# Value products of an attention kernel moved to 64x64 and 32-row tiles of the TensorE array, with smaller weight casts in the ramp

## The chip, the cores and the metric

The kernel runs on one core of a Trainium2 chip. The metric is device time in microseconds (us) of one execution, as median of several; the profile of one of them gives the span, which is about 1.7 us shorter.

## The reference

Eight batches, eight heads, 576 queries, head dimension 64. K and V are averaged over eight neighbours, which leaves 72 keys per head; the attention's output goes through a two-layer MLP of width 2048.

```python
k_p = k.reshape(B, H, Sp, 8, D).mean(axis=3)          # Sp = 72
v_p = v.reshape(B, H, Sp, 8, D).mean(axis=3)
attn = softmax(q @ k_p^T / sqrt(D))
x = (attn @ v_p), heads side by side                  # 4608 x 512
out = gelu_tanh(x @ w_in) @ w_out                     # w_in 512 x 2048, w_out 2048 x 512
```

## The kernel before

Tokens come in nine groups of 512: groups 0 to 7 hold 512 queries of one batch each, and a remainder group R holds the last 64 of every batch; it runs before group 7. TensorE works through group g's MLP while the attention of the next group is slipped in between, at numbered slots ("hooks"). The eight heads' 72 weights each lie side by side in 576 rows, cut into five chunks of 128, the first of which is half empty, so a head's rows straddle two chunks. The pooled V (`vbd`) is stored once for every pair of heads and chunk, with a mask that zeroes the rows of other heads. One pair's value product is then two full-array matmuls, most of whose rows are zeros or other heads' blocks:

```python
PARTS = {0: [(0, 0), (1, 1)], 1: [(1, 2), (2, 3)], 2: [(2, 4), (3, 5)], 3: [(3, 6), (4, 7)]}  # (chunk, vbd slot)

def values(g, half, eng):                     # called twice per group: half 0, then half 1
    xo = psum.tile([128, 2, MAIN], F32, name="xo", tag="sc", bufs=2)
    for i in range(2):
        pr = 2 * half + i
        for x, (c, n) in enumerate(PARTS[pr]):            # groups 1 to 7
            nc.tensor.matmul(out=xo[:, i, :], lhsT=vbd[:, g, n, :], rhs=eT[:, :, c, :],
                             start=(x == 0), stop=(x == 1))
        # ... (remainder group: 64 columns at a time)
    copy(eng, st[g]["xT"][:, 2 * half:2 * half + 2, :], xo)      # eng is ScalarE

def hidden(g, fo, hook, s):                   # 16 per group
    for ko in range(KO):                                  # KO = 4 slices of xT
        hook(s + ko)
        nc.tensor.matmul(out=hp, lhsT=w_in_b[:, ko, ...], rhs=st[g]["xT"][:, ko, :], ...)
    nc.scalar.activation(out=gT[:, fo, :], in_=hp, func=ACT.Gelu_apprx_tanh)
```

Here `eT` holds a group's transposed softmax weights, `xo` its value products and `xT` their copy that the MLP reads; `kbd`, met later, is its pooled K as the score matmuls read it. After a group's value products come the last output matmuls of the group before (four for group 1, seven for the others), and then `hidden` reads `xT`. The ramp (group 0 and the first weights) is a chain of its own: warm-up matmuls, pooling of K by TensorE (`vp`), scores, softmax on VectorE, value products in halves, and GpSimd casting w_in as it lands. In the ramp, the slots are

```python
warm_up(34, "mm")
# ...
at(hooks, 80, cast_q, 1, 0, 2, nc.gpsimd)     # group 1's q, the half that is transposed first
at(hooks, 80, cast_q, 1, 2, 4, nc.vector)
# ...
at(hooks, [114, 118, 122, 125][j], q_transpose_pe, 1, j, nc.vector, "sc")
```

The softmax here doesn't subtract the row's maximum and nothing guards it: scores larger than these inputs give would overflow.

## Time and profile before

| | before |
|---|---|
| median of the first 3 runs | 298.57 us |
| span of the profiled run | 296.90 us |
| TensorE busy | 288.5 us, 97% |
| value products, groups 1 to 7 | 56 matmuls, 1.73 us of path per group |
| stretch from one group's value products to the next | 29.72 (group 1), 30.35 (groups 2, 3, 5), 30.48 (group 4) |
| TensorE's longest waits in the ramp, once its warm-up has begun at 1.43 us | 0.81 us for the K transfer, 0.79 and 0.69 for VectorE's softmax, 0.48 and 0.23 for w_in casts |

"Stretch" is the measure to follow: from the first value matmul of a group to that of the next. The lines themselves stand in the prediction. In them PE is TensorE and PEld its weight loads, DVE is VectorE, ACT ScalarE, POOL GpSimd, and SPq the queue of SyncE, which issues transfers.

### The profile page before, as it was taken

Reading aid. Unit: us, or ns where it says so; the run is one execution under the profiler, and the core shown is the slowest. Engines: PE = TensorE matmul, PEld = TensorE weight load, DVE = VectorE, ACT = ScalarE, POOL = GpSimd, SP = SyncE. Lnnn points to the kernel's source line nnn. Section 1 sums busy time; section 2 is a strip of 40 time slices with the busy share of each in tenths; the row PEclk is TensorE's granted clock in tenths of the full one; section 3 lists DMA queues with packets and bytes.
Section 4 is the critical chain, followed back from the end, with each engine's and each line's share of the span. In section 5 each row is a group of like instructions: output and inputs, shape, how many; then the busy total and the mean of one; then the engine's idle time right before and its main releaser. Section 6 shows DMA issues by size and latency. Waiting matters only on the chain.

```text
span 296.9 us, 4533 instructions
## 1 busy us (share of the span) xinstructions
PE 288.5 (97%) x1716; PEld 149.3 (50%) x1716; DVE 140.3 (47%) x234; ACT 155.9 (52%) x229; POOL 63.3 (21%) x82
## 2 busy tenths in 40 slices
PE   6889999999999999999999999999999999999996
PEld 6668854445444544454445444544444544444445
DVE  5873768165527561747065807481729100920012
ACT  1475584777066706671567256724773367427500
POOL 3564433231303040304002400240024000100000
PEclk9999999999999999999999999999999999999999
DMA  7999997995699269936994599059944600451012
GB/s 235 356 386 342 382 365 204 345 253 156 139 307 299 58 137 290 264 112 135 276 257 148 125 265 288 1 116 249 278 143 102 167 36 2 83 111 35 2 71 71
DMA packets 73301, 56.32 MB, mean 190 GB/s; under 512 B 45888, under 2 KB 55488, under 8 KB 73280
## 3 DMA queue, kind: packets, MB, share of 16 engines
q1 hardware_dynamic: 73136, 55.98, 67.9%
q8 instruction: 13, 0.21, 0.3%
q10 hardware_dynamic: 144, 0.07, 0.1%
q14 instruction: 8, 0.07, 0.1%
HBM read 36.70 MB, written 9.44 MB: 155 GB/s over the span
## 4 chain that ended last, share of the span: by engine, by line
PE 91%; DMA 4%; SPq 3%; POOL 1%; issue 0%; DVE 0%
PE mm L326 41%; PE mm L310 37%; PE xo L280 4%; PE mm L321 4%; DMA w_in_s<-in_moe_w_in_dram 4%; PE sc L213 2%; SPq L403 2%; PE mm L354 1%; POOL w_in_b L80 1%; SPq L98 1%; PE xo L286 1%; SPq L110 0%; PE sc L220 0%; PE tp L198 0%; PE xo L269 0%
## 5 line engine op out<-in xcount | busy, mean ns | idle before, releaser
L326 PE MATMUL mm<-w_out_b,gT 128*128 128x512 bf16 x560 | 128.7, 379 | 0.0
L310 PE MATMUL mm<-xT,w_in_b 128*128 128x512 bf16 x512 | 111.8, 379 | 0.0
L312 ACT ACTIVATE gT<-mm 128x512 bf16<-128x512 f32 x128 | 76.5, 597 | 41.8 <-PE mm L310 41.8
L326 PEld LDWEIGHTS <-gT 128*128 128x128 bf16 x560 | 53.4, 98 | 58.5
L310 PEld LDWEIGHTS <-w_in_b 128*128 128x128 bf16 x512 | 50.1, 98 | 60.5
L80 DVE COPY osb<-mm 128x512 f32<-128x512 f32 (+2 forms) x37 | 24.2, 658 | 60.9 <-PE mm L326 58.7
L78 ACT CAST xT<-xo 128x1024 bf16<-128x1024 f32 (+1 forms) x18 | 16.6, 967 | 57.5 <-PE xo L280 47.8
L235 DVE TENSOR_REDUCE den<-e 128x8 f32<-128x576 f32 x36 | 26.5, 736 | 41.6 <-ACT e L228 41.6
L153 POOL TENSOR_TENSOR vbd<-kvb,vmask 128x256 bf16<-128x256 bf16 (+2 forms) x40 | 21.2, 553 | 104.9 <-DVE kvb L133 104.7
L131 DVE TENSOR_TENSOR kv<-kv 128x1024 f32<-128x1024 f32 (+3 forms) x19 | 21.8, 1147 | 33.8 <-DMA kv<-in_v_dram 30.0
L228 ACT ACTIVATE e<-sc 128x576 f32<-128x576 f32 x36 | 22.4, 650 | 9.7 <-ACT e L228 5.8
L240 DVE TENSOR_TENSOR eb<-e,r 128x576 bf16<-128x576 f32 x26 | 24.4, 940 | 0.9
L80 POOL CAST q_b<-q_sb 128x2048 bf16<-128x2048 f32 (+2 forms) x9 | 17.1, 1897 | 14.6 <-DMA q_sb<-in_q_dram 8.5
L240 POOL TENSOR_TENSOR eb<-e,r 128x576 bf16<-128x576 f32 x6 | 6.9, 1149 | 61.3 <-ACT e L228 34.1
L321 PE MATMUL mm<-xT,w_in_b 128*128 128x256 bf16 x128 | 15.9, 273 | 0.7 <-POOL w_in_b L80 0.7
L213 PEld LDWEIGHTS <-qT 128*128 128x128 bf16 x128 | 10.0, 98 | 7.2 <-issue 0.4
L213 PE MATMUL sc<-kbd,qT 128*128 128x144 bf16 x128 | 13.1, 226 | 0.3 <-ACT qT L78 0.2
L321 PEld LDWEIGHTS <-w_in_b 128*128 128x128 bf16 x128 | 12.0, 98 | 2.6 <-POOL w_in_b L80 1.3
L280 PE MATMUL xo<-eT,vbd 128*128 128x512 bf16 x56 | 13.2, 379 | 0.0
L132 DVE TENSOR_TENSOR kv<-kv 128x512 f32<-128x512 f32 (+3 forms) x19 | 12.4, 651 | 0.7
L323 ACT ACTIVATE gT<-mm 128x512 bf16<-128x512 f32 x16 | 9.4, 597 | 5.2 <-PE mm L321 5.2
L520 ACT ACT_TABLE_LOAD x8 | 10.3, 1283 | 0.1
(59 smaller groups left out, 124.7 us busy)
## 6 DMA issues: line engine op xcount, KB each, us to landing
out_dram<-osb SPq DMA_DIRECT2D x31, 256.0 KB, 6.7
kv<-in_k_dram SPq DMA_DIRECT2D x7, 1024.0 KB, 7.4
q_sb<-in_q_dram SPq DMA_DIRECT2D x7, 1024.0 KB, 6.3
kv<-in_v_dram SPq DMA_DIRECT2D x6, 1024.0 KB, 8.9
w_in_s<-in_moe_w_in_dram SPq DMA_DIRECT2D x8, 512.0 KB, 10.4
w_out_s<-in_moe_w_out_dram SPq DMA_DIRECT2D x4, 1024.0 KB, 13.7
kv<-in_v_dram SPq DMA_DIRECT2D x4, 512.0 KB, 10.2
out_dram<-osb SPq DMA_DIRECT2D x9, 128.0 KB, 2.3
```

The costliest lines, as they stand in the source:

```text
L80: eng.tensor_copy(out=out, in_=in_)
L131: add(out=t[:, :, 0:4, :], in0=t[:, :, 0:4, :], in1=t[:, :, 4:8, :], op=ALU.add)
L153: eng.tensor_tensor(out=vbd[p0:128, b, n0:n1, :].rearrange("p (c r) (hh d) -> p c (r hh) d", c=max(m, 1), d=D), in0=kvb[p0:128, 4 + c0:4 + ...
L213: nc.tensor.matmul(out=o, lhsT=qT[:, j, pr, :], rhs=kbd[:, g, pr].rearrange("d hh s -> d (hh s)"), start=True, stop=True)
L228: nc.scalar.activation(out=e.rearrange("p (x h) s -> p x (h s)", x=2), in_=sc[:, :, 0:4 * Sp], func=ACT.Exp, scale=1.0 / 64.0)
L235: nc.vector.reduce_sum(out=den, in_=e, axis=AX.X)
L240: eng.tensor_tensor(out=o.rearrange("p (h s) -> p h s", s=Sp), in0=e, in1=r.unsqueeze(2).to_broadcast([128, H, Sp]), op=ALU.mult)
L280: nc.tensor.matmul(out=xo[:, i, :], lhsT=vbd[:, g, n, :], rhs=eT[:, :, c, :], start=(x == 0), stop=(x == 1))
L310: nc.tensor.matmul(out=hp, lhsT=w_in_b[:, ko, fo * 128:(fo + 1) * 128], rhs=st[g]["xT"][:, ko, :], start=(ko == 0), stop=(ko == KO - 1))
L312: nc.scalar.activation(out=gT[:, fo, :], in_=hp, func=ACT.Gelu_apprx_tanh)
L321: nc.tensor.matmul(out=hp[:, f, :], lhsT=w_in_b[:, ko, (fo + f) * 128:(fo + f + 1) * 128], rhs=st[g]["xT"][:, ko, c0:c0 + 256], start=(ko ...
L326: nc.tensor.matmul(out=o, lhsT=gT[:, fo, r * 128:(r + 1) * 128], rhs=w_out_b[:, fo, :], start=(fo == 0), stop=(fo == FO - 1))
```

## The change

The intent is to use the array's empty part. A head's 72 rows are split in a block of at most 64 rows and a rest of at most 32, at row offsets that the array can take as a tile; sixteen small matmuls then replace eight large ones, and four on different tiles can run side by side. Smaller w_in casts and earlier slots for group 0's second value products are meant to shorten TensorE's waits in the ramp.

```diff
+    BIG = [(64, 0), (0, 1), (64, 1), (0, 2), (0, 3), (64, 3), (0, 4), (64, 4)]        # per head: first row, chunk
+    SMALL = [(0, 1), (64, 1), (0, 2), (64, 2), (96, 2), (32, 3), (96, 3), (32, 4)]
-    def values(g, half, eng):
+    def values(g, eng):
+        xo = [psum.tile([128, 2, MAIN], F32, name="xo", tag="sc", bufs=2) for _ in range(2)]
+            for part, rows_ in ((SMALL, 32), (BIG, 64)):
+                for i in range(2):
+                    for pr in (i, i + 2):
+                        for hh in range(2):
+                            r0, c = part[2 * pr + hh]
+                            n = dict(PARTS[pr])[c]
+                            nc.tensor.matmul(out=xo[i][64 * hh:64 * hh + 64, pr // 2, :],
+                                             lhsT=vbd[r0:r0 + rows_, g, n, 64 * hh:64 * hh + 64],
+                                             rhs=eT[r0:r0 + rows_, :, c, :], start=(part is SMALL), stop=(part is BIG))
 ... (remainder group: as before, pairs in the order 0, 2, 1, 3)
+            copy(eng, st[g]["xT"].rearrange("p (y i) t -> p i y t", i=2)[:, i], xo[i])
 ...
-        for ko in range(KO):
+        for i, ko in enumerate([0, 2, 1, 3]):
 ...
-        cast_w_in(c, 2, nc.gpsimd)
+        cast_w_in(c, 2, nc.gpsimd, 0, 256)
+        cast_w_in(c, 2, nc.gpsimd, 256, 512)
 ...
-    at(hooks, 32, first_t, 3)
-    at(hooks, 38, first_v)
+    at(hooks, 26, first_t, 3)
+    at(hooks, 32, first_v)
```

More of the change, by code (lines that the diff above doesn't have):

```diff
@@ L271, in values_half @@
         copy(eng, st[g]["xT"][:, 2 * x:2 * x + 2, 256 * half:256 * half + 256], xo)
-    def values(g, half, eng):
-        xo = psum.tile([128, 2, MAIN], F32, name="xo", tag="sc", bufs=2)
+    BIG = [(64, 0), (0, 1), (64, 1), (0, 2), (0, 3), (64, 3), (0, 4), (64, 4)]
+    SMALL = [(0, 1), (64, 1), (0, 2), (64, 2), (96, 2), (32, 3), (96, 3), (32, 4)]
+    def values(g, eng):
+        xo = [psum.tile([128, 2, MAIN], F32, name="xo", tag="sc", bufs=2) for _ in range(2)]
         eT = st[g]["eT"]
-        for i in range(2):
-            pr = 2 * half + i
-            if g < B:
-                for x, (c, n) in enumerate(PARTS[pr]):
-                    nc.tensor.matmul(out=xo[:, i, :], lhsT=vbd[:, g, n, :], rhs=eT[:, :, c, :],
-                                     start=(x == 0), stop=(x == 1))
-            else:
-                for b in range(B):
-                    p0 = 64 * (b % 2)
-                    for x, (c, n) in enumerate(PARTS[pr]):
-                        nc.tensor.matmul(out=xo[:, i, 64 * b:64 * b + 64], lhsT=vbd[:, b, n, :],
-                                         rhs=eT[:, b // 2, c, p0:p0 + 64], start=(x == 0), stop=(x == 1))
-        copy(eng, st[g]["xT"][:, 2 * half:2 * half + 2, :], xo)
@@ new lines, in values @@
+        if g < B:
+            for part, rows_ in ((SMALL, 32), (BIG, 64)):
[7 more added lines that the diff above has]
+                                             rhs=eT[r0:r0 + rows_, :, c, :], start=(part is SMALL), stop=(part is BIG))
+        else:
+            for i in range(2):
+                for pr in (i, i + 2):
+                    for b in range(B):
+                        p0 = 64 * (b % 2)
+                        for x, (c, n) in enumerate(PARTS[pr]):
+                            nc.tensor.matmul(out=xo[i][:, pr // 2, 64 * b:64 * b + 64], lhsT=vbd[:, b, n, :],
+                                             rhs=eT[:, b // 2, c, p0:p0 + 64], start=(x == 0), stop=(x == 1))
@@ L307, in hidden @@
         hp = psum.tile([128, MAIN], F32, name="mm", tag="mm", bufs=4)
-        for ko in range(KO):
-            hook(s + ko)
+        for i, ko in enumerate([0, 2, 1, 3]):
+            hook(s + i)
             nc.tensor.matmul(out=hp, lhsT=w_in_b[:, ko, fo * 128:(fo + 1) * 128],
-                             rhs=st[g]["xT"][:, ko, :], start=(ko == 0), stop=(ko == KO - 1))
+                             rhs=st[g]["xT"][:, ko, :], start=(i == 0), stop=(i == KO - 1))
         nc.scalar.activation(out=gT[:, fo, :], in_=hp, func=ACT.Gelu_apprx_tanh)
@@ L405, with cast_w_in @@
                 in_=moe_w_in[128 * k0:128 * k0 + 256, 512 * c:512 * c + 512].rearrange("(ko p) f -> p ko f", p=128))
-    def cast_w_in(c, k0, eng):
+    def cast_w_in(c, k0, eng, f0=0, f1=512):
         o = 512 * (c % 2)
-        copy(eng, w_in_b[:, k0:k0 + 2, 512 * c:512 * c + 512], w_in_s[c // 2][:, k0:k0 + 2, o:o + 512])
+        copy(eng, w_in_b[:, k0:k0 + 2, 512 * c + f0:512 * c + f1], w_in_s[c // 2][:, k0:k0 + 2, o + f0:o + f1])
     w_out_s = {}
@@ L524, in tail_of_attention @@
         at(hooks, va, nc.scalar.preload_act_table_set, GELU_SET)
-        at(hooks, va, values, n, 0, nc.scalar)
-        at(hooks, va, values, n, 1, nc.scalar)
+        at(hooks, va, values, n, nc.scalar)
     hooks = {}
     at(hooks, 16, first_t, 2)
-    at(hooks, 32, first_t, 3)
-    at(hooks, 38, first_v)
+    at(hooks, 26, first_t, 3)
+    at(hooks, 32, first_v)
     at(hooks, 72, pool, 1, 0, 4)
```

## The prediction

> **What bounds the kernel now.** I read the page first, then the chain of waits in order of time, then the stretches from one group's value products to the next one's, then the ramp as a timeline. The page's first table and its releasers say that TensorE is the bound and hardly ever waits:
>
> ```profile
> PE 288.5 (97%) x1716; PEld 149.3 (50%) x1716; DVE 140.3 (47%) x234; ACT 155.9 (52%) x229; POOL 63.3 (21%) x82
> ...
> L280 PE MATMUL xo<-eT,vbd 128*128 128x512 bf16 x56 | 13.2, 379 | 0.0
> ```
>
> The reader is to see PE at 97%, and the line that the change rewrites: 56 matmuls, eight in each of seven groups, no idle time before them. 379 ns is one matmul's latency; they start 0.216 us apart. The chain shows what eight of them cost and what lies around them:
>
> ```profile
> 80.28 1.73 PE xo L280 x8
> 82.01 1.51 PE mm L326 x7
> 83.52 13.81 PE mm L310 x64
> ```
>
> So a group's value products are 1.73 us of path, followed by seven output matmuls of the group before (1.51 us) and then by the first matmuls that need xT. Stretch by stretch PE is busy from end to end:
>
> ```profile
> core 0: us, PE busy (x) PEld busy (x) DVE busy (x) ACT busy (x) POOL busy (x), PEclk, DMA share, GB/s
> 50.40:80.12 29.72, 29.72 (x151) 13.99 (x149) 15.40 (x25) 17.03 (x25) 8.01 (x9) 1.00 0.82 230
> 140.82:171.30 30.48, 30.48 (x153) 14.24 (x152) 15.47 (x24) 16.54 (x24) 6.02 (x7) 1.00 0.82 201
> ```
>
> Here (group 1 and group 4) us equals PE busy; only one stage stops it a little: in group 4's stretch the first score matmul starts at 158.65 where its neighbours' pace puts it at 158.52.
>
> The 64x64 tiles of the change are already in this kernel, in the scores of the remainder group:
>
> ```profile
> 219.44 0.21 PEld L220 LDWEIGHTS <-qT 64*64 64x64 bf16 x16 [0.42 <-issue]
> 219.44 0.33 PE L220 MATMUL sc<-kbd,qT 64*64 64x72 bf16 x16
> 219.70 0.60 PE L326 MATMUL mm<-w_out_b,gT 128*128 128x512 bf16 x2
> ```
>
> Sixteen matmuls of 72 columns pass in 0.26 us from start to start. One after another at full-array pace (0.0625 us for the 144 columns of the ordinary scores, so about 0.031 for 72) they would take 0.50. Single records give the pieces: they start in four rounds of four, within a round 3 to 4 ns apart, rounds at 219.444, .498, .532 and .563. A round thus lasts about 0.032, the time of one matmul, and the first 0.022 more. The last full-array matmul before starts at 219.135 and streams 0.216, so entering costs 219.444 - 219.351 = 0.093. Leaving costs 219.702 - 219.563 - 0.032 = 0.107.
>
> **What the Trainium skill says.** "TensorEngine Tiling (Array Packing)", section Key Properties: tiles load and multiply independently, and "Changing tiling mode (not just tile) drains the TensorE". The trace agrees: four tiles at once, about 0.1 us at each change. "TensorE: Matmul & The Clock Gate", section The mechanism, puts starts of concurrent tiles about 4 ns apart; here 3 to 4. The Tiling page's Restrictions say that column tiling turns off fast weight load; here a 64-column load took 102 to 111 ns against 98 for the 128-column group, so no gain from its halved width, but the loads lay beside the rounds except for the 0.022. "PSUM — Partial Sum Buffer", section PSUM bank collisions raise a hardware error, lets tiles write one bank if the quadrants differ. The new order keeps each round of four to distinct (bank, half of the partitions), so I expect correct results; no record here shows two row tiles in one bank.
>
> **The change part by part.** (1) Value products, groups 1 to 7. Removed: 8 x 0.216 = 1.73 us. Added: 16 matmuls of the same 512 columns, eight in 32-row tiles and then eight in 64x64 tiles. Each eight are two rounds of four on four different tiles, if the order of the compiled program is kept (it is: I read it). Each round streams 0.216. Sum: enter 0.093, first load 0.022, two rounds 0.432, change from 32 to 64 rows about 0.100 (an estimate, the mean of enter and leave), load 0.022, two rounds 0.432, leave 0.107: 1.21. Saved per group on PE: 0.52. Seven would make 3.6, but not all reach the end.
>
> (2) What follows them. xT leaves by two ACT copies, which in groups 2 to 7 before end 2.08 and 2.99 us after the value products' start; ACT had been idle before the first:
>
> ```profile
> 81.18 1.93 ACT L78 CAST xT<-xo 128x1024 bf16<-128x1024 f32 x2 [7.28 <-PE xo L280]
> ```
>
> Before, the first copy could start when four matmuls were done, at 0.647 + 0.379 = 1.03. Now its tile is done with the first 64x64 round, which starts at 0.093 + 0.022 + 0.432 + 0.100 = 0.647: about 1.05 with the load. So xT comes no earlier: 2.10 and 3.01, against hidden matmuls that come 0.52 earlier. The new order of the hidden products (ko 0, 2, 1, 3) uses the first copy's two slices first, so the third matmul is the one that needs the second copy. In groups 2 to 7 it is due at 1.21 + 1.51 + 0.43 = 3.15: free, by 0.1. In group 1 only four output matmuls follow, so it is due at 1.21 + 0.86 + 0.43 = 2.50 and waits until about 3.03, where the kernel before needed its second copy at 3.02. Group 1 gains nothing.
>
> (3) The next group's scores (a stretch is named after the group whose value products open it). They come 17.70 us after the value products' start if PE doesn't wait; they need kbd, which VectorE finishes (last copy's end, same origin) at 16.00, 15.51, 16.17, 17.68, 16.30, 14.66 in the stretches of groups 1 to 6. It hangs on the K transfer, which is issued around the value products and so doesn't follow a faster PE. With scores due at 17.18, only group 4's stretch stops, by some 0.6; if its transfer lands as late as before, its 0.52 is all lost. I count half of it. The transposed softmax weights land 0.3 to 0.5 before the value products, but their chain starts at scores of the same stretch and shifts with them.
>
> (4) The ramp. Weight pieces, and value products six slots earlier. Before, PE waited 0.23 and 0.48 us for w_in casts (the page's 0.7) around 21.1 and 23.8. Pieces halve a cast that took about 1.04 to 1.6, and PE should be some 0.6 ahead by 25 us. But it can't keep that:
>
> ```profile
> 32.42 1.54 POOL L80 CAST q_b<-q_sb 128x1024 bf16<-128x1024 f32 x1 [6.10 <-ACT gT L323]
> ...
> 34.01 0.40 PE L198 MATMUL tp<-identb,q_b 128*128 128x128 bf16 x4
> ```
>
> The q load of group 1 landed at 32.27 by the DMA's records, POOL began at once (the releaser named is long done), and PE's transpose followed the cast's end, 33.96, after waiting 0.085. This is a transfer's time in a stretch where the DMA engines are 90% busy or more, so the 0.6 becomes idle time ahead of 34.01. Worth: 0. The three extra POOL instructions are beside the path too: a 512-column cast takes 0.61 by the w_out casts, so a split costs 2 x 0.61 - 1.04 = 0.19.
>
> Sum: groups 2, 3, 5, 6 and 7: 5 x 0.52 = 2.6; group 4: 0.25; group 1 and the ramp: 0. The remainder group keeps its full-array matmuls. 298.57 - 2.85 = 295.7.
>
> **Rivals.** (a) Everything arrives: 7 x 0.52 + 0.6 = 4.2, 294.3. For it: PE is 97% of the span. Against: the three arrivals above, each read from a record. The xT copies cap it as well: the third hidden matmul was at 3.24 + 0.43 = 3.67 and can't come before about 3.05, so 0.62 a group even with free tile changes, 6 x 0.62 = 3.7, 294.8. (b) The 512-column matmuls don't overlap as the 72-column ones did, for instance because four moving operands or weight loads share something: with rounds half as fast, value products take about 2.1 and the kernel loses 0.35 x 7 = 2.5, 301. For it: no record shows 32-row tiles, or 512 columns in tiles. Against: the 72-column rounds ran at one matmul's pace. (c) Changes of tile size cost more, say 0.2 each: 1.5 per group, gain 0.2 x 6, 297.3. (d) K or q transfers collide differently and another stretch stops at kbd: minus 0.3 to 0.5 each.
>
> **Range and chances.** The point is 295.7. The lower edge, 294.5, is rival (a)'s cap and a little; the upper, 297.4, rival (c). Over 2% faster would need 5.97 us, more than the cap; that leaves 3%. Slower by 2% needs tiles that hardly overlap (16 x 0.216 = 3.46 a group, plus 12 us): 3%.
>
> **What would show each step.** The chain's value stage should read about 1.2 in place of 1.73, in four rounds with three gaps of 0.1. Hidden matmuls' third should wait for ACT xT about 0.5 in group 1 alone. The first scores after group 4 should wait for VectorE's kbd about 0.6. PE should idle some 0.5 before 34.0, and the value stage of group 1 should start at 50.4 as before. Wrong would be: value stages far from 1.2, group 1's start well before 50.2, or waits in other stretches.

## The result

| | before | after |
|---|---|---|
| median | 298.63 us (298.57 to 298.78, 4 runs) | 296.45 us (295.68 to 297.05, 4 runs) |
| ratio | | 0.9925, 95% interval 0.9901 to 0.9949 |
| span of the profiled run | 296.90 us | 294.59 us |

Ratios here and below are the mean time of one kernel's runs over that of the other's runs of the same rounds, so they are not quite the ratio of the medians. The gain is clear of noise and below 2%. What strikes is the spread: the first four runs of before lie within 0.21 us, those of after within 1.37.

The first table of the page and, from the groups, the rewritten line of the kernel after:

```profile
PE 286.2 (97%) x1772; PEld 147.1 (50%) x1772; DVE 140.5 (48%) x234; ACT 156.0 (53%) x229; POOL 64.2 (22%) x85
...
L290 PE MATMUL xo<-eT,vbd 32*64 32x512 bf16 (+1 forms) x112 | 8.3, 387 | 0.0
```

There are twice as many value matmuls, and their busy time (overlaps counted once) fell from 13.2 to 8.3 us. TensorE is as full as before. Its chain of waits in order of time, for the value products of group 2 and what follows (columns: start us, us, what):

```profile
81.00 1.11 PE xo L290 x16
82.11 1.62 PE mm L340 x7
83.73 13.81 PE mm L324 x64
```

The stage is 1.11 us where it was 1.73; but the seven output matmuls behind it now read 1.62 and not 1.51, because the time to leave the small tiles is put down to them. Single records give the stage as predicted: the last full-array matmul starts at 80.625 and streams 0.216; rounds of four start at 80.934, 81.174, 81.488 and 81.728; the next full-array matmul starts at 82.046. From 80.841 to 82.046 is 1.205 us. Entering costs 0.093, changing from 32 to 64 rows 0.098, leaving 0.102, and the first round of each size is 0.024 longer. Within a round the records start 3 to 4 ns apart.

The stretches of the kernel after, from group 1's value products on (columns: window, length, and per engine busy time and number of instructions, then the granted clock, DMA share and GB/s):

```profile
51.17:80.93 29.76, 29.44 (x158) 13.44 (x157) 15.30 (x25) 17.04 (x25) 7.94 (x9) 1.00 0.82 229
80.93:110.78 29.85, 29.85 (x163) 13.75 (x162) 15.08 (x24) 16.54 (x24) 6.02 (x7) 1.00 0.83 204
110.78:140.77 29.99, 29.99 (x162) 13.66 (x161) 15.72 (x24) 16.54 (x24) 6.03 (x7) 1.00 0.83 204
140.77:170.61 29.84, 29.84 (x161) 13.74 (x160) 15.53 (x24) 16.54 (x24) 6.03 (x7) 1.00 0.77 204
```

Groups 2 and 4 take 29.84, 0.51 and 0.63 less than before. Group 3 takes 29.99: its scores waited 0.15 for kbd. The chain has it as 0.40 where the other groups' first four score matmuls have 0.25:

```profile
127.39 0.65 PE mm L340 x3
128.03 0.40 PE sc L213 x4
```

Group 1 takes 29.76, as much as before (29.72), and TensorE is busy for only 29.44 of it. And group 1 starts at 51.17, where it started at 50.40. This last is the surprise: 0.77 us lost in a ramp that was to be worth nothing. TensorE's timeline of the first microseconds shows where; first the kernel before, then after:

```profile
4.71 0.48 PE L437 MATMUL warm<-identb 128*128 128x128 bf16 x3
6.00 2.02 PE L140 MATMUL vp<-kv,identf 128*128 128x128 f32 x16 [0.81 <-DMA kv<-in_k_dram]
7.86 0.28 PE L179 MATMUL kT<-identb,kvb 128*128 128x128 bf16 x2
```

```profile
4.71 0.53 PE L451 MATMUL warm<-identb 128*128 128x128 bf16 x3
5.96 3.75 PE L140 MATMUL vp<-kv,identf 128*128 128x128 f32 x16 [0.72 <-DMA kv<-in_k_dram]
9.50 0.45 PE L179 MATMUL kT<-identb,kvb 128*128 128x128 bf16 x3
```

Up to here the two kernels issue the same TensorE instructions. The same sixteen pooling matmuls took 2.02 us in one trace and 3.75 in the other. The clock records say why: full speed was granted 5.01 us after the start in before's trace and at 9.57 in after's. The whole softmax chain of group 0 hangs on those matmuls.

A ledger of the two profiled spans: group 1's start +0.77, its stretch +0.04, groups 2 to 5 -0.51, -0.36, -0.63 and -0.51, from group 6's value products to the end -1.12. That is -2.32, against a measured -2.31. Was the ramp's +0.77 the change's fault, or chance? That is what the first experiments ask.

### The profile page after: what moved, and what is told of

Its sections match the earlier page's. It is cut to its first block, busy times and chain, and to the rows that moved or that the text cites. A ratio compares the mean times of both kernels' runs of the same rounds, so it can differ in the third digit from the quotient of the medians. Undisturbed runs are those within 1.5% of the kernel's fastest.

```text
span 294.6 us, 4648 instructions
## 1 busy us (share of the span) xinstructions
PE 286.2 (97%) x1772; PEld 147.1 (50%) x1772; DVE 140.5 (48%) x234; ACT 156.0 (53%) x229; POOL 64.2 (22%) x85
## 4 chain that ended last, share of the span: by engine, by line
PE 92%; DVE 3%; DMA 2%; ACT 1%; issue 0%; SPq 0%
PE mm L340 41%; PE mm L324 37%; PE mm L335 4%; PE xo L290 3%; PE sc L213 2%; DMA kv<-in_k_dram 2%; PE vp L140 1%; PE mm L368 1%; DVE eb L240 1%; DVE den L235 1%; ACT xT L78 1%; PE xo L269 1%; PE xo L299 1%; PE tp L198 0%; PE sc L220 0%; PE tp L254 0%
## 5 line engine op out<-in xcount | busy, mean ns | idle before, releaser
L80 DVE COPY kbd<-kTd 64x288 bf16<-64x288 bf16 x12 | 5.0, 413 | 8.6 <-DMA kTd<-kvb 8.5
```

Source lines behind the costliest of these rows:

```text
L80: eng.tensor_copy(out=out, in_=in_)
```

## The experiments

Twelve kernels ran, in three calls, each call on one chip with its own runs of the kernel before (medians 298.77, 298.76 and 298.95 us).

**The changed kernel again, and its two parts alone.** `after_again` is unchanged.

> The changed kernel once more, unchanged, for the spread of its runs. In the first trace TensorE's full clock was granted at 9.57 us after the span's start, against 5.01 us in the kernel before, and the sixteen fp32 pooling matmuls took twice as long. Theory A (the late grant delays the ramp, by chance from run to run): runs fall between 295.5 and 297.1 us; a profile with the grant near 5 us has group 1's value products at 50.4 us and reads 0.8 us less than 296.3, one with the grant near 9.5 us has them at 51.2. Theory B (the changed ramp itself costs 0.8 us): group 1's value products start at 51.2 whatever the grant.

Measured: 296.14 us median (295.57 to 296.93, 5 runs), ratio 0.9908 (0.9893 to 0.9924). Its profile fell on an early grant, 5.74 us: the pooling matmuls took 2.02 us, group 1's value products started at 50.58, and that run took 295.57. So theory A's condition is met to 0.2 us. The kernel before, too, now spread from 298.52 to 299.29 over nine runs; its first four were lucky. In this trace nothing waited for kbd, and the spans can be compared at an early grant on both sides: 293.85 against 296.90, group 1's start +0.18, its stretch +0.04, groups 2, 3 and 5 -0.51 each, group 4 -0.63, from group 6 on -1.12: -3.06, measured -3.05.

TensorE's timeline where group 1's q is transposed shows what became of the ramp's gain:

```profile
33.09 0.49 PE L335 MATMUL mm<-xT,w_in_b 128*128 128x256 bf16 x3
34.11 0.40 PE L198 MATMUL tp<-identb,q_b 128*128 128x128 bf16 x4 [0.53 <-POOL q_b L80]
```

It stood idle for 0.53 us until GpSimd's cast of q, which ended at 34.05. In the kernel before it waited less than 0.1 there.

`tiles_only` has the tiles with the ramp of before:

```diff
-        cast_w_in(c, 2, nc.gpsimd, 0, 256)
-        cast_w_in(c, 2, nc.gpsimd, 256, 512)
+        cast_w_in(c, 2, nc.gpsimd)
-    at(hooks, 26, first_t, 3)
-    at(hooks, 32, first_v)
+    at(hooks, 32, first_t, 3)
+    at(hooks, 38, first_v)
```

> The tiles and the new order of the hidden products, with the ramp of the kernel before (whole w_in casts, first value products six slots later). Theory A (the ramp part is worth nothing, as group 1's q cast bounds it): 295.6 with an early clock grant, 296.0 with a late one; within 0.4 us of the changed kernel in the mean, and per group the same 29.84 us. Theory B (the ramp part costs 0.8 us): 295.5 and no spread. If the ramp part gains 0.6: 297.

Measured: 295.83 us (295.76 to 296.52, 4 runs), ratio 0.9904 (0.9890 to 0.9917). `ramp_only` is the kernel before with those same lines changed the other way:

> The kernel before with the changed ramp alone. Theory A: 298.6 with an early clock grant (TensorE idles about 0.5 us more just before the first q transposes at 34.0 us), up to 299.4 with a late one. Theory B (the changed ramp costs 0.8 us by itself): 299.4 in all runs. If the pieces gain what they were meant to: 298.0.

Measured: 298.82 us (298.61 to 299.20, 5 runs), ratio 1.0003 (0.9989 to 1.0017). So all of the gain is that of the tiles and the new order of the hidden products that goes with them (the order was not run alone), and the ramp part is worth nothing that these rounds can tell. Its trace had the clock at 5.30 us and group 1's value products at 50.45, against 50.40: the changed ramp does not cost 0.8 us by itself, and theory B falls. It had 0.65 us of idle time ahead of the first q transposes. I had also expected the ramp part to hurt by some 0.3 us when the grant is late; the runs are too few to say.

**The clock grant.** `warm42` fills the idle time before the pooling matmuls with more warm-up:

```diff
-    warm_up(34, "mm")
+    warm_up(42, "mm")
```

> The changed kernel with 42 instead of 34 warm-up matmuls, which fill TensorE's idle time from 5.0 to 5.96 us while it waits for K. Theory A: the stretch of uninterrupted work grows, [...]the runs draw together below 296.2, median 295.7. Theory B (spread and delay have nothing to do with the clock grant): same spread and median as the changed kernel, 296.4.

Measured: 295.82 us (295.64 to 296.22, 4 runs), ratio 0.9900 (0.9887 to 0.9914). The grant came at 6.72 us and the pooling took 2.40 us. Against 0.9908 for `after_again` in the same rounds the gain is not clear of noise; the spread narrowed from 1.36 to 0.58 us. None of the four traces with 42 warm-up matmuls has a grant after 6.72 us, but four are few. `warm8` does the opposite, with `warm_up(8, "mm")`:

> The changed kernel with 8 instead of 34 warm-up matmuls, so that the clock can hardly be granted before the pooling matmuls at 5.96 us have run. Theory A (the late grant makes the slow runs): the sixteen pooling matmuls take 3.7 us instead of 2.0, group 1's value products start at 51.2 or later, all runs between 296.3 and 297.2. Rival (the slow runs come from transfers): a spread as the changed kernel has, from 295.6.

Measured: 298.00 us (297.29 to 298.59, 6 runs), ratio 0.9964 (0.9951 to 0.9978). All runs are slower than the slowest of the changed kernel on any chip here, and by more than expected. The timeline of its start:

```profile
1.43 1.03 PE L451 MATMUL warm<-identb 128*128 128x128 bf16 x8 [1.43 <-POOL identb masks.py:199]
6.27 3.56 PE L140 MATMUL vp<-kv,identf 128*128 128x128 f32 x16 [3.80 <-DMA kv<-in_k_dram]
```

The grant was at 9.50 us, the pooling matmuls took 3.56 us, and group 1's value products started at 51.74. The rest of its loss lies later and was not expected. The stretches of groups 1 and 4 are 30.19 and 30.39 us: counted from the stretch's start, kbd was ready at 17.30 in group 1's (16.11 in `after_again`), and the last transposed softmax weights landed at 30.18 in group 4's (29.43). The remainder group's value stage took 0.67 us more, since its last transposed weights landed 0.98 us after it had begun. A late grant is thus seen with a start of group 1 that is 0.6 us later (`after` against `after_again`, 51.17 against 50.58) to 1.2 us later (`warm8`); part of the 1.2 may be K's, since the pooling began at 6.27 and not at 5.84. No trace of the kernel before has a late grant. That it also shifts the transfers into worse meetings is only argued. Late grants also turned up in the traces of `qswap` (pooling 3.75 us; it has no clock record) and `phases` (granted at 9.84). The Trainium skill, "TensorE: Matmul & The Clock Gate", section What's actually happening, says that the gate is judged in free-running windows of about 3.4 us, so that the moment varies from run to run. The traces agree: with 34 warm-up matmuls it came at 5.00, 5.01, 5.30, 5.74, 5.94, 7.38 (a trace with only 0.45 us of idle time before the pooling), 9.57 and 9.84. The window itself shows too: in the thirteen traces with clock records, full speed lasted 286.72, 290.13 or 293.55 us, which differ by steps of 3.41 and are 84, 85 and 86 of them.

**What the value stage costs.** `phases` splits the two phases into four:

```diff
-            for part, rows_ in ((SMALL, 32), (BIG, 64)):
-                for i in range(2):
+            for i in range(2):
+                for part, rows_ in ((SMALL, 32), (BIG, 64)):
```

> The changed kernel with the value products in four phases instead of two: 32-row tiles and then 64x64 tiles for the first output tile, then both again for the second. The same sixteen matmuls in the same four rounds, but two more changes of tile size. If each change costs what the records of the changed kernel show (0.098 us and 0.024 for the first load), the stage takes 1.45 us instead of 1.205 and the stretches of groups 2, 4 and 5 30.09 instead of 29.84; group 1, whose first copy starts 0.2 earlier, gains back about 0.2; in sum 1.2 us slower, 297.3. If the gaps were something else (first use of a tile, for instance), 296.1.

Measured: 297.34 us (296.83 to 297.51, 4 runs), ratio 0.9941 (0.9928 to 0.9954). TensorE's timeline of group 2's stage:

```profile
80.48 0.38 PE L340 MATMUL mm<-w_out_b,gT 128*128 128x512 bf16 x1
80.79 1.43 PE L290 MATMUL xo<-eT,vbd 32*64 32x512 bf16 x16
82.15 0.39 PE L340 MATMUL mm<-w_out_b,gT 128*128 128x512 bf16 x1
```

From the last full-array matmul's end of streaming at 80.697 to the next at 82.149 is 1.452 us, predicted 1.45; the stretches of groups 2 to 5 are 30.09; group 1's is 29.55, so it gained 0.22. A change of tile size costs about 0.12 with the slower first round, each time, and not once.

`pairs_alike` keeps two phases but puts two matmuls in a row on the same tile:

```diff
-                for i in range(2):
-                    for pr in (i, i + 2):
-                        for hh in range(2):
+                for hh in range(2):
+                    for pr in range(4):
+                        for i in (pr % 2,):
```

> The changed kernel with the same sixteen value products in another order, two in a row on the same tile of the array. If overlap of different tiles is what gains (theory A), each eight take five rounds of 0.216 instead of two: the stage takes 2.50 us instead of 1.205, the stretches of groups 2 to 5 are 31.14 instead of 29.84, and the time is 305, slower than before. If only the smaller tile shapes matter, whatever the order: 296.

Measured: 296.74 us (1 run). My expectation missed by over 8 us, and taken by its letter the result is the other case's, that the order doesn't matter. The value stage took 1.226 us, hardly more than 1.205, and TensorE's timeline shows no trace of five rounds:

```profile
80.21 0.38 PE L340 MATMUL mm<-w_out_b,gT 128*128 128x512 bf16 x1
80.52 1.20 PE L290 MATMUL xo<-eT,vbd 32*64 32x512 bf16 x16
81.65 0.39 PE L340 MATMUL mm<-w_out_b,gT 128*128 128x512 bf16 x1
```

In single records four matmuls start together, at 80.517, .524, .530 and .537, and the next four from 80.757 on. They are 6 to 7 ns apart where neighbours on different tiles were 3 to 4 ns apart, as if each second one had been passed over. Their semaphores show that it was: the program puts the wait for a free output tile on its first and second matmul, and in the records it stands on the first and the fifth to start; the completion signal of the fifteenth stands on the fourth record of the 64-row phase, at 81.101. (The compiled program keeps the order of the source.) That signal came only at 81.753, and the sixteenth's at 81.787: the starts left the program's order, the signals of completion did not. So a matmul whose tile is busy does not hold up a later one on a free tile. The overlap theory itself isn't refuted, since sixteen times 512 columns in 1.2 us need it; but what I derived from it, strict program order of starts, is wrong. I could not build a version without any overlap to test the theory from the other side. This order has a cost elsewhere: both output tiles are now signalled together, the first xT copy ends at 2.27 instead of 2.03 us after the stage's start, and the stretches are 30.01 instead of 29.84.

A version with all sixteen in 64x64 tiles, which would save one change of size, was not run. Each head's two products come from different row tiles and add into the same half of a bank, and with one tile size nothing orders them. The changed kernel: in its trace the first 64x64 round starts 0.314 us after the second 32-row round, 0.098 more than that round streams, so the change of size keeps the two apart. What the version would be worth stays open.

**The two losses that the prediction named.** `dve1` lets VectorE make the second xT copy in group 1:

```diff
-            copy(eng, st[g]["xT"]...[:, i], xo[i])
+            copy(nc.vector if g == 1 and i == 1 else eng, st[g]["xT"]...[:, i], xo[i])
```

> The changed kernel with the second xT copy of group 1 on VectorE beside the first on ScalarE. Theory A (group 1 gains nothing because its two serial xT copies end at 2.94 us after the value products' start): its third hidden matmul comes at about 2.6 instead of 2.99, the stretch of group 1 shrinks from 29.77 by 0.3 to 0.45 us, and the median falls as much, to 295.8. Rival (VectorE is held by output copies there): no change or a loss of up to 0.3.

Measured: 295.55 us (295.44 to 296.09, 4 runs), ratio 0.9895 (0.9882 to 0.9907). ScalarE's and VectorE's copies in its timeline, then TensorE's hidden matmuls:

```profile
51.80 1.01 ACT L78 CAST xT<-xo 128x1024 bf16<-128x1024 f32 x1 [4.21 <-PE xo L290]
...
52.02 1.23 DVE L80 CAST xT<-xo 128x1024 bf16<-128x1024 f32 x1 [0.43 <-PE xo L290]
...
52.87 1.46 PE L324 MATMUL mm<-xT,w_in_b 128*128 128x512 bf16 x6
```

The copies run side by side, and the stretch of group 1 is 29.29 us, 0.48 less than 29.77, a little over the expected range. (The stretch is the evidence; the ratio's interval overlaps that of the changed kernel.)

`qswap` exchanges the engines of the two q casts of group 1:

```diff
-    at(hooks, 80, cast_q, 1, 0, 2, nc.gpsimd)
-    at(hooks, 80, cast_q, 1, 2, 4, nc.vector)
+    at(hooks, 80, cast_q, 1, 0, 2, nc.vector)
+    at(hooks, 80, cast_q, 1, 2, 4, nc.gpsimd)
```

> The changed kernel, with VectorE casting the half of group 1's q that is transposed first (0.7 us) and GpSimd the other (1.5 us), the other way round from now. Theory A (the ramp's gain is there, but waits for GpSimd's cast of q until 34.0 us): the idle time of 0.53 us ahead of the first q transposes goes, group 1's value products start about 0.5 us earlier (50.1 against 50.58 at an early clock grant), and the median falls by 0.4 to 0.5, to 295.7. Rival (the next arrival, the second half of q or the pooled V, holds it at the same place): no change, 296.1.

Measured: 296.41 us (295.18 to 297.33, 6 runs), ratio 0.9919 (0.9901 to 0.9937). By itself this is inconclusive: the profiled run had the slow pooling of a late grant, so TensorE reached the q transposes at 35.07 us, long after either cast. Only the fastest run, 295.18, hints at a gain. Hence two more kernels with 42 warm-up matmuls. `warm42_qswap`:

> The changed kernel with 42 warm-up matmuls and q's first half cast by VectorE. With the late grants out of the way, the swap shows alone against the 295.8 of 42 warm-up matmuls: theory A (GpSimd's cast of q eats the ramp's gain) says 295.3, no idle time ahead of the first q transposes and group 1's value products near 50.3 instead of 50.85; the rival (another arrival holds it) 295.8.

Measured: 295.36 us (295.04 to 295.81, 4 runs), ratio 0.9878 (0.9863 to 0.9892), against 295.82 and 0.9900 for `warm42`. TensorE's timeline:

```profile
33.13 0.83 PE L335 MATMUL mm<-xT,w_in_b 128*128 128x256 bf16 x6
33.80 0.39 PE L198 MATMUL tp<-identb,q_b 128*128 128x128 bf16 x4
```

The idle time before the transposes is gone, where `warm42` had 0.54; group 1's value products start at 50.26 instead of 50.85. (The intervals of the two ratios overlap and the two grants differ, 4.37 and 6.72 us; the vanished wait is the firmer evidence.) `before_warm42_qswap` makes the same two edits in the kernel before:

> The kernel before with the same two edits. Its ramp reaches the first q transposes only 0.1 us before the cast is done, so the swap has nothing to gain there: 298.6, at most 0.2 below the kernel before, and the runs above 299 gone. If the two edits were worth as much as in the changed kernel, 297.9.

Measured: 298.59 us (298.49 to 299.16, 5 runs), ratio 0.9991 (0.9979 to 1.0003). As expected, the median is 298.6 and the edits do little here, though 0.36 us by the medians where at most 0.2 was expected; and one run of 299.16 shows that 42 warm-up matmuls don't end the spread.

**All three.** `best` is the changed kernel with 42 warm-up matmuls, the q casts exchanged and group 1's second copy on VectorE.

> The changed kernel with all three: 42 warm-up matmuls, q's first half cast by VectorE, group 1's second xT copy on VectorE. If the three losses add up (theory A): 0.4 for the grant, 0.5 for q and 0.4 for the copy, so 294.9 and a spread below 0.6. If what one wins another takes (the pooled V of group 1 is ready only at 50.5): 295.4.

Measured: 294.50 us (294.29 to 294.69, 4 runs), ratio 0.9854 (0.9840 to 0.9868) to the kernel before in the same rounds. It beats both kernels, and comes out 0.4 below the expected 294.9. Against the early-grant trace of `after_again` the span is 0.90 us shorter: group 1's value products start 0.43 earlier and its stretch is 0.48 shorter, so what the two edits win adds up. Its chain of waits around group 1's value products:

```profile
41.16 9.06 PE mm L340 x42
50.22 1.11 PE xo L290 x16
51.33 0.97 PE mm L340 x4
52.30 13.90 PE mm L324 x64
```

No copy is in the chain any more, where the chain of the changed kernel had, at the same place:

```profile
51.24 0.92 PE xo L290 x12
52.16 0.02 issue
52.18 1.94 ACT xT L78 x2
54.12 0.04 issue
54.16 13.54 PE mm L324 x62
```

## Why the prediction was right

The measured 296.45 lies in the range of 294.5 to 297.4, and the point of 295.7 was 0.75 us too fast; later rounds gave 296.14. Part of the nearness is luck, since two misses offset each other: counted at an early grant on both sides, the groups from 2 on gave 3.28 us where 2.85 was summed, and the ramp and group 1 lost 0.22 where 0 was; in the result's own trace they gave 3.13 and lost 0.81.

**Value stage (step 1): right to a hundredth.** 1.205 us measured against 1.21 worked out from sixteen 72-column matmuls of another stage. The assumed change from 32 to 64 rows was 0.098 (0.100 estimated), and 512 columns overlapped as 72 did, which disposes of rivals (b) and (c). `phases` confirmed the price of a change by adding two. (The starts within a round of those other matmuls are 2 to 5 ns apart in the records, not 3 to 4; nothing rests on it.)

**The copies (step 2): right.** In group 1 the third hidden matmul starts 0.48 us after its turn, at 2.99 us after the first value matmul; that is 3.09 from the end of the matmul before, from which the prediction counts its 3.03. And the stretch did not shrink. `dve1` showed that the copy was the cause by taking it off ScalarE. In the other groups nothing waits for the copies.

**The scores (step 3): the mechanism was right, its place and size were off.** I took group 4's K transfer "as late as before" and counted 0.25 us lost. In the new traces kbd in group 4's stretch was ready 16.13 and 16.61 us after the value products' start, not 17.68, so group 4 lost nothing and even won back the 0.12 that it lost before. The stall showed up in group 3 instead, a wait in another stretch, which the prediction had named as a sign of being wrong: 0.15 us in the first trace, 0.09 in `tiles_only`, 0.24 in `dve1`, none in `after_again`. The term of 0.25 is some 0 to 0.24, and not tied to a group. One trace gives a transfer's arrival to no better than a microsecond.

**The ramp (step 4): right about q, incomplete about the start.** The pieces and earlier slots did put TensorE ahead, and with an early grant (`after_again`) it waited 0.53 us for GpSimd's cast of q, foretold as "some 0.5"; in the result's own trace, with a late one, it came to the transposes at 34.70, after the cast, and didn't wait. `warm42_qswap` made that gain real by moving the cast. "Worth: 0" held for the edits alone (`ramp_only`, ratio 1.0003). The step that failed is that group 1 "should start at 50.4 as before": the ramp was read from one trace whose clock was granted at 5.01 us, and I took its pace as fixed. With grants at 9.5 us and later, group 1 of the changed kernel started 0.6 us later and more. That can be most of the difference between the point and the median, for the run of `after_again` with an early grant took 295.57; the grants of the runs without a trace are not on record.

Rival (a), that everything arrives, would have been 294.3. It took three more edits to get near it, at 294.50.

## What to carry to other kernels

As seen here, small tiles of the array pay when four independent products can be laid on four different tiles and the stage is long enough for the price of the changes, here 0.3 us for a stage that fell from 1.73 to 1.2; group the products by tile size, and let the change order those that add into one place. A saving on the bounding engine arrives only up to the next arrival, so list the arrival times of every operand (copies, casts, transfers) beside the new due times before summing; moving two such arrivals to another engine was worth about as much as two groups' tiles. Before taking one trace's ramp as the kernel's, look when the full clock was granted in it.

## What the Trainium skill lacked or had wrong

- "TensorE: Matmul & The Clock Gate", The mechanism, says that matmuls start strictly in program order. `pairs_alike` doesn't agree: with two in a row on the same tile, four tiles still ran together, and the stage took 1.226 us where ordered starts would need 2.50. Completion was still signalled in program order. 4 ns between concurrent starts is right (3 to 4 ns in the value rounds of the changed kernel).
- "TensorEngine Tiling (Array Packing)", Key Properties, says that a change of tiling mode drains the array, but not what it costs: 0.093 us from full array to 32x64, 0.098 from 32x64 to 64x64, 0.102 back to the full array, and 0.022 to 0.024 more for the first round of each.
- The same page, section Gotcha 1: PSUM Pressure, says that different row tiles can't access the same PSUM bank at once. Here row tiles at rows 0 and 64 (and 96 and 32) wrote the two halves of one bank at the same time, at full pace and with correct results. "PSUM — Partial Sum Buffer", section PSUM bank collisions raise a hardware error, quotes the same ban, but measured the error only for row tiles that meet in one bank and quadrant, which no round does here.
- No page says outright that a change of tiling mode can stand in for the ordering of two row tiles that add into one place. The changed kernel relies on it, with 0.098 us between the phases and correct results in all runs.
- "TensorE: Matmul & The Clock Gate", What's actually happening, has the free-running window and puts the cost below one per cent of a span. That holds here, but the page lacks what it means for comparing two tuned kernels: after a late grant sixteen fp32 matmuls took 3.75 instead of 2.02 us and group 1 started 0.6 us later or more. That is 0.2% of the time, but a fifth of this change's gain of 3.05 us at like grants, and two traces can fall on different sides of it.
